# Attention, mixture of experts and MLP in one kernel: laying out keys and queries once per pair of heads

## The chip, the cores and the metric

The kernel runs as one program on one core of a Trainium2 chip. The metric is the device time of one execution in microseconds. The profile is of one execution, and its times are counted from the first instruction of the program (the span).

## What is computed

Three layers follow one another. The first is what the change is about: attention over 4 batches of 8 heads with 1152 keys and half as many queries, since neighbouring queries are averaged first.

```
q, k, v: (4, 8, 1152, 64) float32
q_pool = q.reshape(B, H, S // 2, 2, D).mean(axis=3)
scores = matmul(q_pool, k.T) / sqrt(D)
attn   = exp(scores - max(scores)); attn /= sum(attn) + 1e-9
out    = matmul(attn, v)
```

Its output, heads side by side, is x (4, 576, 512). Then x goes through four attention experts of 64 columns each (causal, with weights wq, wk, wv, wo and a gate that picks two of the four), and at last through a mixing step with U and V and an MLP of 512 to 2048 to 512 with residual.

## The kernel before

**Pairs.** Two heads are handled together, their 2 x 64 columns side by side on the 128 partitions: 16 pairs in all. For a pair, `prep` (L499) makes what its scores need. `load_q`, `load_k`, `load_v` (L477 to L497) fetch raw rows into `qr`, `kr`, `vr`. `pool_q` adds neighbouring queries on VectorE (DVE). `tr_q` turns the queries on TensorE (PE) in two pieces (4 and 2 transposes), `tr_k` the keys in three pieces of three transposes. Each turned piece is split into a high part (`qh`, `kn`, by ScalarE, ACT) and a remainder (`ql`, `klo`, by DVE). `evac_q_all` (L383) and `evac_k` (L354) then copy the parts by DMA, piece by piece, into the operands of the score matmuls: keys into `s1a, s1b, s2a, s2b`, queries into `q1a, q1b, q2a, q2b`, and the queries also into `bd`, a block-diagonal form. A class `Pair` holds the eight score operands; there are two Pairs, for even and odd pairs of heads, and two each of `bd` and `kn`. A row maximum is needed before the scores: `mxs` (L527) multiplies `bd` by `kn` on PE (27 matmuls per pair) and reduces each on DVE into `mp`; `fin` (L540) turns the maxima and puts them by small DMAs (`nm`, L423) into a row of `q2a` and `q2b`, once for queries 0 to 319 and once for the rest.

**Steps.** `attend` (L53) writes the order by hand for PE, DVE and ACT. A pair has 18 units (2 halves of the queries x 9 key tiles), a unit two steps: 36 steps per pair. A step issues two score matmuls (L566, L567) and the exponential on ACT (L568, `pt`). Every third unit the value matmuls (L586) of earlier units follow. GpSimd (POOL) sums the `pt` tiles (L578). Into these steps, by the numbers of the tables at L20 to L27, the preparation of the next pair is placed: number 0 is the first step of the pair that runs just before, number 36 the first of the pair itself. What a step returns as a function is run one step later.

**Queues.** All DMAs are issued by one engine, SP, one after another. Their order is not written by hand: a scheduler sets it, from the order of the code and its own estimate of when their inputs are ready. If an instruction at SP's head waits, all that stand behind it wait.

**Weights.** `expert_weights` (L256) loads the experts' weights into halves of one staging tile `stg` (L278 to L321) and cuts them into high and low parts (`cut`, L226: ACT, then DVE). The six loads are spread over the odd pairs 1, 3, 5, 7, 9, 11: the load at step 7 of the pair (`WL_AT`), the cuts at steps 17 and 29 and, where there are more than two, again in the next pair (`WC_AT`).

**First and last pair.** Before the loop, all of pair 0's preparation is run by `run_all` (L611), in the order of its numbers; pair 1's is placed into the first steps of pair 0 (L626). During the last pair the first expert's preparation takes the free places (L893 to L895): the pool of the attention's right side is closed, four cuts of x (`xh`, `xl`, L227 and L228) and 15 steps of projections (L669) and maxima are spread evenly from step 12 on.

After the attention come the experts (same structure, 8 pairs of batch and expert pair) and the MLP (L922 to L1052), neither of which the change edits beyond renaming an argument.

Of the kernel before, what the change touches and what calls it, by code (L numbers as in the profile page):

```python
# [18 lines left out]

GROUP = 3  # L20
POOL_AT, LQ_AT, LK_AT, V_AT = -13, -48, -24, 6
Q_AT = [-1, 5]
K_AT = [-1, 5, 11]
M_AT = [1, 2, 3, 6, 7, 8, 9, 12, 13, 14, 15, 16, 18, 19, 20, 21, 22, 24, 25, 26, 27, 30, 31, 32, 33, 36, 37]
F_AT = [23, 41]

WL_AT, WC_AT = 7, [17, 29]  # L27


CUT_AT = [0, 0, 0, 0]  # L30
# [98 lines left out]
def kernel(  # L129
# [45 lines left out]
    def f(ap):  # L175
        return ap.bitcast(F32)
# [177 lines left out]
    def evac_k(klo, ps, kn, pr, sl):  # L354


        nc.scalar.activation(kn[:, sl], ps, AF.Copy)

        def rest():
            nc.vector.tensor_sub(klo, ps, f(kn[:, sl]))  # L360
            for a in range(2):
                for h in range(2):
                    nc.sync.dma_start(f(pr.S1[a][HALF[h], sl]), f(kn[HALF[a], sl]))
                nc.sync.dma_start(f(pr.S2[a][HALF[a], sl]), f(klo[HALF[a]]))

        return rest

    def evac_q(ps, bd, pr, sl, done):
        t0, nt = sl.start // 64, (sl.stop - sl.start) // 64
        for a in range(2):  # L370
            nc.scalar.activation(pr.Q1[a][HALF[a], sl], ps[HALF[a]], AF.Copy)

        def rest():
            for a in range(2):
                nc.vector.tensor_sub(pr.Q1[a][HALF[1 - a], sl], ps[HALF[a]], f(pr.Q1[a][HALF[a], sl]))
                nc.sync.dma_start(f(pr.Q2[a][HALF[a], sl]), f(pr.Q1[a][HALF[a], sl]))
                nc.scalar.activation(bd[HALF[a], t0:t0 + nt, HALF[1 - a]],
                                     ps[HALF[a]].rearrange("p (t j) -> p t j", j=64), AF.Copy)
            done()

        return rest

    def evac_q_all(qh, ql, ps, bd, pr, sl, done):  # L383


        t0, nt = sl.start // 64, (sl.stop - sl.start) // 64
        nc.scalar.activation(qh, ps, AF.Copy)

        def rest():
            nc.vector.tensor_sub(ql, ps, f(qh))  # L390
            for a in range(2):
                r = HALF[a]
                nc.sync.dma_start(f(bd[r, t0:t0 + nt, r]), f(qh[r]).rearrange("p (t j) -> p t j", j=64))
            for a in range(2):
                r = HALF[a]
                nc.sync.dma_start(f(pr.Q1[a][r, sl]), f(qh[r]))
                nc.sync.dma_start(f(pr.Q1[a][HALF[1 - a], sl]), f(ql[r]))
                nc.sync.dma_start(f(pr.Q2[a][r, sl]), f(qh[r]))
# [100 lines left out]
    def prep(i):  # L499
# [9 lines left out]
        def tr_k(c):  # L509
            kr = kraw[i]  # L510
            ps = pst.tile([P, 512], F32, name="st") if i == 0 else pms.tile([P, 512], F32, name="ms")
            for j in range(3):
                nc.tensor.transpose(ps[:, j * P:(j + 1) * P], kr[:, 3 * c + j, :, :], ident)
            sl = slice(c * 384, c * 384 + 384)
            own["k", c, i % 2] = i
            return evac_k(per_r.tile([P, 384], F32R, name="klo", bufs=2), ps[:, :384], KN[i % 2], pr, sl)

        def tr_q(j0, j1):
            ps = pms.tile([P, 512], F32, name="ms")
            n = (j1 - j0) * 96  # L520
            for j in range(j0, j1):
                nc.tensor.transpose(ps[:, (j - j0) * 96:(j - j0 + 1) * 96], st["qp"][:, j, :, :],
                                    ident[:96, :96])
            qh, ql = (per_r.tile([P, 384], F32R, name=nm) for nm in ("qh", "ql"))
            return evac_q_all(qh[:, :n], ql[:, :n], ps[:, :n], BD[i % 2], pr, slice(j0 * 96, j1 * 96), lambda: own.update({(t, i % 2): i for t in range(j0 * 96 // 64, j1 * 96 // 64)}))

        def mxs(t, c):  # L527
            assert own[t, i % 2] == i and own["k", c, i % 2] == i
# [24 lines left out]
    def unit(i, u):  # L553
# [51 lines left out]

        return score, pv, (post_a, post_r, post_b) if kt == NKT - 1 else None

    load_q(0)
    load_k(0)
    load_v(0)  # L610
    run_all(sorted(prep(0), key=lambda x: x[0]))  # L611
    n = 4 * NKT
    for x, (load, steps) in enumerate(expert_weights()):
        place(side, [(WL_AT, load)], n * (1 + 2 * x))
        at = [y + n * w for w in range(2) for y in WC_AT]
        place(side, list(zip(at, steps)), n * (1 + 2 * x))
        assert len(steps) <= len(at)
    for i in range(NP):
        units += [unit(i, u) for u in range(2 * NKT)]
    for i in range(1, NP):  # L620
        n0 = (i - 1) * n
        for at, g in ((LQ_AT, load_q), (LK_AT, load_k), (V_AT, load_v)):
            side.setdefault(max(3 * i - 3, n0 + at), []).append(lambda g=g, i=i: g(i))
        for at, g in prep(i):
            if i == 1:
                at = max(at, 2 if at == POOL_AT else 5 if at in Q_AT + K_AT else 6)  # L626
            side.setdefault(n0 + at, []).append(g)
# [83 lines left out]
    def prep_b(j, what):  # L711
# [372 lines left out]
```

## Time and profile before

| | |
|---|---|
| median of 3 runs | 1261.41 us (1260.43 to 1265.64) |
| the profiled execution | 1257.52 us, span 1255.7 us |
| before the first exponential | 36.1 us |
| attention, first full score to the last pair's end | about 35.5 to 594.6 us |
| PE busy | 1141.4 us, 91% of the span |
| DVE, ACT, POOL busy | 61%, 37%, 39% |
| DMA | 120.06 MB, mean 96 GB/s |

A pair's start is read in the timeline as its first score matmul (L566; 36 of them make a pair); from pair to pair that gives the stretches used below. A busy PE is not PE at its peak, since matmuls overlap, so the idle time of PE in a stretch says more than its busy share. The column PEclk is the mean granted clock of TensorE in the stretch, 1.00 being 2.4 GHz.

### The profile page before, as it was taken

The numbers are of one execution on the slowest core, as the hardware profiler recorded it, in microseconds if no ns is written. First come the engines' busy times: TensorE is split into PE (matmuls) and PEld (weight loads), VectorE is DVE, ScalarE is ACT, GpSimd is POOL, SyncE is SP. The second block draws the span as 40 slices with busy tenths as digits, with TensorE's granted clock in tenths as the row PEclk, the third lists the DMA queues.
The fourth block names the chain that finished last, engine by engine and source line by source line (L and its number), as shares of the span: only waits on it lengthen the run. The fifth ranks groups of instructions, "written<-read, shape, count | busy, mean of one in ns | idle before, by whom it ended". The sixth has DMA issues, their size and how long they took to land.

```text
span 1255.7 us, 19444 instructions
## 1 busy us (share of the span) xinstructions
PE 1141.4 (91%) x6748; PEld 909.8 (72%) x6748; DVE 766.8 (61%) x1661; ACT 468.0 (37%) x1184; POOL 488.1 (39%) x382
## 2 busy tenths in 40 slices
PE   4696999798989788998999999999999999999998
PEld 3474676566767566766877777578897898998987
DVE  5264676477778568665675858998849228222222
ACT  1253455355545445554445454542221112111110
POOL 4274777477767657784222212421112003000000
PEclk9997999899999989998999999999999999999999
DMA  7556666647575656521120404435303002000111
GB/s 172 123 122 141 156 147 148 145 115 182 128 177 138 157 116 149 137 65 39 39 65 13 110 5 114 135 122 206 101 18 110 8 1 68 1 1 1 51 51 50
DMA packets 140000, 120.06 MB, mean 96 GB/s; under 512 B 76288, under 2 KB 123392, under 8 KB 139904
## 3 DMA queue, kind: packets, MB, share of 16 engines
q1 hardware_dynamic: 139904, 118.84, 37.5%
q8 instruction: 53, 0.87, 0.3%
q14 instruction: 43, 0.35, 0.1%
HBM read 52.65 MB, written 9.44 MB: 49 GB/s over the span
## 4 chain that ended last, share of the span: by engine, by line
PE 56%; DVE 19%; issue 11%; DMA 6%; ACT 3%; SPq 3%; POOL 1%; ACTq 0%; DVEq 0%; POOLq 0%
PE ms L990 9%; PE pv L586 9%; PE o L1001 8%; PE ms L669 6%; PE st L566 5%; PE ms L533 5%; PE st L567 4%; DVE mp L535 3%; DMA bd<-qh 2%; PE pv L817 2%; DVE dca L238 1%; DVE dcb L246 1%; ACT pt L568 1%; DVE dca L241 1%; PE st L792 1%
## 5 line engine op out<-in xcount | busy, mean ns | idle before, releaser
L578 POOL TENSOR_TENSOR acc<-acc,pt 128x576 f32<-128x576 f32 x224 | 326.7, 1459 | 102.2 <-ACT pt L568 75.4
L568 ACT ACTIVATE pt<-st 128x288 f32<-128x288 f32 x576 | 218.0, 409 | 213.2 <-PE st L567 197.0
L535 DVE TENSOR_REDUCE mp<-ms 128x1 f32<-128x384 f32 x432 | 213.9, 547 | 69.0 <-PE ms L533 68.8
L990 PE MATMUL ms<-uh,w 128*128 128x384 f32 x768 | 214.4, 340 | 0.8 <-DVE hl L994 0.8
L533 PE MATMUL ms<-kn,bd 128*128 128x384 f32 x432 | 156.9, 374 | 45.8 <-DVE mp L535 18.0
L1001 PE MATMUL o<-w,hh 128*128 128x512 f32 x576 | 182.1, 396 | 2.1 <-ACT hh L993 2.1
L994 DVE SCALAR_TENSOR_TENSOR hl<-ms,hh 128x384 fp32r<-128x384 f32 x96 | 53.4, 556 | 199.2 <-ACT hh L993 198.8
L586 PE MATMUL pv<-pt,vr 128*64 128x288 f32 x1152 | 165.9, 425 | 0.0
L990 PEld LDWEIGHTS ms<-uh,w 128*128 128x128 f32 x768 | 140.9, 188 | 6.0 <-DVE hl L994 1.0
L993 ACT ACTIVATE hh<-ms 128x384 fp32r<-128x384 f32 x96 | 46.8, 489 | 262.7 <-PE ms L990 262.7
L990 PE MATMUL ms<-ul,w 128*128 128x384 f32 x384 | 129.7, 338 | 2.2 <-DVE ul L228 2.2
L533 PEld LDWEIGHTS ms<-kn,bd 128*128 128x128 f32 x432 | 85.7, 199 | 59.6 <-DVE mp L535 29.0
L228 POOL TENSOR_TENSOR w<-dcb,w 128x512 fp32r<-128x512 f32 x32 | 43.7, 1369 | 214.8 <-ACT w L227 206.5
L586 PEld LDWEIGHTS pv<-pt,vr 128*64 128x64 f32 x1152 | 79.3, 141 | 59.0 <-issue 16.1
L1001 PEld LDWEIGHTS o<-w,hh 128*128 128x128 f32 x576 | 106.8, 188 | 21.0 <-ACT hh L993 3.4
L1001 PE MATMUL o<-w,hl 128*128 128x512 f32 x288 | 114.2, 396 | 1.7 <-DVE hl L994 1.7
L566 PE MATMUL st<-q1b,s1b 128*128 128x288 f32 x288 | 88.1, 306 | 18.3 <-ACT pt L568 18.2
L566 PE MATMUL st<-q1a,s1a 128*128 128x288 f32 x288 | 98.6, 342 | 0.7 <-ACT pt L568 0.7
L566 PEld LDWEIGHTS st<-q1a,s1a 128*128 128x128 f32 x288 | 55.6, 193 | 46.0 <-issue 42.2
L567 PE MATMUL st<-q2a,s2a 128*128 128x288 f32 x288 | 86.7, 301 | 1.8 <-issue 1.8
L567 PE MATMUL st<-q2b,s2b 128*128 128x288 f32 x288 | 86.9, 302 | 0.0
L809 POOL TENSOR_TENSOR acc<-acc,pt 128x576 f32<-128x576 f32 (+4 forms) x48 | 44.2, 920 | 108.8 <-ACT pt L800 104.7
(169 smaller groups left out, 1890.9 us busy)
## 6 DMA issues: line engine op xcount, KB each, us to landing
raw<-in_moe_w_ch_dram SPq DMA_DIRECT2D x32, 512.0 KB
qr<-in_q_dram SPq DMA_DIRECT2D x16, 576.0 KB
vr<-in_v_dram SPq DMA_DIRECT2D x16, 576.0 KB
s1a<-kn SPq DMA_DIRECT2D x96, 96.0 KB
s1b<-kn SPq DMA_DIRECT2D x96, 96.0 KB
kr<-in_k_dram SPq DMA_DIRECT2D x30, 288.0 KB
s2a<-klo SPq DMA_DIRECT2D x48, 96.0 KB
s2b<-klo SPq DMA_DIRECT2D x48, 96.0 KB
```

The lines of the kernel that those rows point to most:

```text
L533: nc.tensor.matmul(ps[:, :384], BD[i % 2][:, t, :], KN[i % 2][:, c * 384:c * 384 + 384], start=True, stop=True)
L535: nc.vector.tensor_reduce(st["mp"][:, t, c:c + 1], ps[:, :384], axis=X, op=ALU.max)
L566: nc.tensor.matmul(ps[:, :HT], pr.S1[a][:, ks], pr.Q1[a][:, qs], start=True, stop=False)
L567: nc.tensor.matmul(ps[:, :HT], pr.S2[a][:, ks], pr.Q2[a][:, qs], start=False, stop=True)
L568: nc.scalar.activation(c["pt"][:, a, :], ps[:, :HT], AF.Exp, scale=0.0625)
L578: nc.gpsimd.tensor_add(acc[i, h], acc[i, h], c["pt"])
L586: nc.tensor.matmul(o[64 * a:64 * a + 64, :HT], vr[:, a, kt, :], c["pt"][:, a, :], start=(kt == 0), stop=(kt == NKT - 1))
L669: nc.tensor.matmul(ps, stat[x][s], mov[x][m], start=(x == 0 and y == 0), stop=(x == n - 1 and y == 2))
L990: nc.tensor.matmul(ps[:, :TB], W[fi][:, 0, a, cs], m[:, c, :], start=(c == 0 and y == 0), stop=(c == NC - 1 and y == 2))
L993: nc.scalar.activation(h, ps[:, :TB], AF.Relu)
L994: nc.vector.scalar_tensor_tensor(l, ps[:, :TB], 0.0, f(h), op0=ALU.max, op1=ALU.subtract)
L1001: nc.tensor.matmul(o[s_], hl[m][:, r], W[fi][:, 1, a, :], start=(fi % FG == 0 and y == 0), stop=(fi % FG == FG - 1 and y == 2))
```

## The change

Four things are edited.

1. **Layout once per pair.** `evac_q_all` is gone. `qh`, `ql` and `klo` become tiles of a whole pair (576, 576 and 1152 columns, one buffer each) in place of pieces of 384. A turned piece now only goes to its staging tile and, for the queries, to `bd`. A new step `lay` at number 13 copies the whole tiles into the eight score operands: 12 DMAs of 64 rows where there were 30. Per pair SP issues 24 DMAs instead of 42: 4 to `bd`, 12 of layout, 4 `nm`, 4 loads (before: 4, 30, 4, 4). The bytes are the same.
2. **Queries turned earlier.** `Q_AT` goes from -1 and 5 to -7 and -1. The first maxima (`M_AT`) start at number 3 instead of 1.
3. **Weight loads.** A load is placed at step 31 of the even pair before, 12 steps earlier than at step 7 of the odd one. The cuts stay where they were.
4. **First and last pair.** Before the loop all turns of pair 0 come first, then the loads of pair 1's keys and queries, then the layout and maxima, then pair 1's own steps with negative numbers. Pair 1's other steps stand at their normal numbers. In the last pair the projections stand at written numbers (`XP_AT`, from 18 on) instead of evenly spread (from 16 on).

```diff
-Q_AT = [-1, 5]
+Q_AT = [-7, -1]
 K_AT = [-1, 5, 11]
-M_AT = [1, 2, 3, 6, 7, 8, 9, 12, 13, 14, 15, 16, 18, 19, 20, 21, 22, 24, 25, 26, 27, 30, 31, 32, 33, 36, 37]
+LAY_AT = 13
+M_AT = [3, 4, 6, 7, 8, 9, 10, 12, 13, 14, 15, 16, 18, 19, 20, 21, 22, 24, 25, 26, 27, 30, 31, 32, 33, 36, 37]
-WL_AT, WC_AT = 7, [17, 29]
+WL_AT, WC_AT = 31, [17, 29]
+XC_AT = [12, 13, 14, 15]
+XP_AT = [18, 19, 21, 22, 25, 26, 27, 28, 29, 30, 31, 32, 33, 34, 35]
...
         def rest():
-            nc.vector.tensor_sub(klo, ps, f(kn[:, sl]))
-            for a in range(2):
-                for h in range(2):
-                    nc.sync.dma_start(f(pr.S1[a][HALF[h], sl]), f(kn[HALF[a], sl]))
-                nc.sync.dma_start(f(pr.S2[a][HALF[a], sl]), f(klo[HALF[a]]))
+            nc.vector.tensor_sub(klo[:, sl], ps, f(kn[:, sl]))
+            if pr:
+                lay_k(klo, kn, pr, sl)
...
+    def lay_k(klo, kn, pr, sl):
+        for a in range(2):
+            for h in range(2):
+                nc.sync.dma_start(f(pr.S1[a][HALF[h], sl]), f(kn[HALF[a], sl]))
+            nc.sync.dma_start(f(pr.S2[a][HALF[a], sl]), f(klo[HALF[a], sl]))
...
-            return evac_k(per_r.tile([P, 384], F32R, name="klo", bufs=2), ps[:, :384], KN[i % 2], pr, sl)
+            return evac_k(klo, ps[:, :384], KN[i % 2], None, sl)
...
-            qh, ql = (per_r.tile([P, 384], F32R, name=nm) for nm in ("qh", "ql"))
-            return evac_q_all(qh[:, :n], ql[:, :n], ps[:, :n], BD[i % 2], pr, slice(j0 * 96, j1 * 96), lambda: own.update({(t, i % 2): i for t in range(j0 * 96 // 64, j1 * 96 // 64)}))
+            if j0 == 0:
+                st["q"] = [per_r.tile([P, T], F32R, name=nm) for nm in ("qh", "ql")]
+            qh, ql = st["q"]
+            sl = slice(j0 * 96, j1 * 96)
+            nc.scalar.activation(qh[:, sl], ps[:, :n], AF.Copy)
+
+            def rest():
+                nc.vector.tensor_sub(ql[:, sl], ps[:, :n], f(qh[:, sl]))
+                for a in range(2):
+                    nc.sync.dma_start(f(BD[i % 2][HALF[a], sl.start // 64:sl.stop // 64, HALF[a]]),
+                                      f(qh[HALF[a], sl]).rearrange("p (t j) -> p t j", j=64))
...
+        def lay():
+
+            qh, ql = st["q"]
+            for a in range(2):
+                nc.sync.dma_start(f(pr.Q1[a][HALF[a]]), f(qh[HALF[a]]))
+                nc.sync.dma_start(f(pr.Q1[a][HALF[1 - a]]), f(ql[HALF[a]]))
+                nc.sync.dma_start(f(pr.Q2[a][HALF[a]]), f(qh[HALF[a]]))
+            lay_k(klo, KN[i % 2], pr, slice(0, S))
...
+    P0, P1 = (sorted(prep(x), key=lambda y: y[0]) for x in range(2))
+    turns = Q_AT + K_AT + [POOL_AT]
     load_q(0)
     load_k(0)
+    run_all([x for x in P0 if x[0] in turns])
+    load_k(1)
+    load_q(1)
     load_v(0)
-    run_all(sorted(prep(0), key=lambda x: x[0]))
+    run_all([x for x in P0 if x[0] not in turns and x[0] < F_AT[1]])
+    run_all([x for x in P1 if x[0] < 0])
+    run_all([x for x in P0 if x[0] == F_AT[1]])
     for x, (load, steps) in enumerate(expert_weights()):
-        place(side, [(WL_AT, load)], n * (1 + 2 * x))
-        at = [y + n * w for w in range(2) for y in WC_AT]
-        place(side, list(zip(at, steps)), n * (1 + 2 * x))
+        place(side, [(WL_AT, load)], n * 2 * x)
+        at = [y + n * w for w in range(1, 3) for y in WC_AT]
+        place(side, list(zip(at, steps)), n * 2 * x)
...
-    steps = sum(prep_b(0, "s"), [])
-    place(side, [(12 + x * (n - 13) / len(steps), g) for x, g in enumerate(steps)], n * (NP - 1))
+    for at, steps in zip((XC_AT, [], XP_AT), prep_b(0, "s")):
+        place(side, list(zip(at, steps)), n * (NP - 1))
```

Where the instructions stand, at the three places that matter. First SP's queue in pair 1, up to the load of the first weights `wq` (four DMAs) into `stg`. Before, from the end of pair 0:

```order
L480 DMA qr<-in_q_dram 96x2x768
L278 DMA stg<-in_moe_wq_dram 128x4x64
L393 DMA bd_135<-qh 64x6x64 x2
...
L363 DMA s1b_142<-kn_139 64x384 x2
L364 DMA s2b_144<-klo 64x384
L496 DMA vr<-in_v_dram 128x2x576
L278 DMA stg<-in_moe_wq_dram 128x4x64 x3
L363 DMA s1a_141<-kn_139 64x384 x2
L364 DMA s2a_143<-klo 64x384
```

With the change:

```order
L469 DMA qr<-in_q_dram 96x2x768
L522 DMA bd_135<-qh 64x6x64 x2
L282 DMA stg<-in_moe_wq_dram 128x4x64 x4
L522 DMA bd_135<-qh 64x3x64 x2
L532 DMA q1a_145<-qh 64x576
L533 DMA q1a_145<-ql 64x576
L411 DMA q2a_161<-nm 1x4x64
```

Before, 31 DMAs of the next pair's `bd` and layout, of `nm` and of `vr` stand between the first and the second DMA of the weights; now all four stand together, ahead of the layout of the pair after.

Second, SP's queue in the same pair from the values' load on, with the change (before, the layout there came in pieces of 64x384 and 64x192, as above):

```order
L485 DMA vr<-in_v_dram 128x2x576
L534 DMA q2a_147<-qh 64x576
L478 DMA kr<-in_k_dram 128x9x64 x2
L532 DMA q1b_146<-qh 64x576
L533 DMA q1b_146<-ql 64x576
L534 DMA q2b_148<-qh 64x576
L373 DMA s1a_141<-kn_139 64x1152 x2
L374 DMA s2a_143<-klo 64x1152
L373 DMA s1b_142<-kn_139 64x1152 x2
L374 DMA s2b_144<-klo 64x1152
L411 DMA q2a_147<-nm 1x5x64
```

The next keys' load `kr` now stands ahead of the keys' layout, where before it stood behind the last piece of it; the maxima `nm` stand behind the whole layout in both.

Third, PE's queue before the loop, up to pair 0's first scores. Before:

```order
L533 MATMUL ms<-kn_139,bd_135 128x384 x10
L418 MATMUL ms<-ident,mx 4x128
L567 MATMUL st<-q2a_147,s2a_143 128x288
...
L522 MATMUL ms<-ident,qp 128x96 x6
L513 MATMUL ms<-ident,kr 128x128 x6
L586 MATMUL pv<-pt,vr 64x288 x2
```

With the change:

```order
L543 MATMUL ms<-kn_139,bd_135 128x384 x10
L576 MATMUL st<-q1a_145,s1a_141 128x288
L511 MATMUL ms<-ident,qp 128x96 x6
L502 MATMUL ms<-ident,kr 128x128 x3
L406 MATMUL ms<-ident,mx 4x128
L577 MATMUL st<-q2a_147,s2a_143 128x288
```

Pair 1's six query transposes and its first three key transposes, which stood behind the first scores of pair 0, now stand ahead of them.

## Rows read from the trace of the kernel before

**Rows 1.** The page: busy time of each engine, share of the span, instructions.

```profile
PE 1141.4 (91%) x6748; PEld 909.8 (72%) x6748; DVE 766.8 (61%) x1661; ACT 468.0 (37%) x1184; POOL 488.1 (39%) x382
```

**Rows 2.** Windows: stretch, length, engines' busy time (instructions), PEclk, DMA share, GB/s.

```profile
0.00:17.00 17.00, 2.79 (x13) 2.42 (x13) 4.92 (x15) 3.24 (x5) 14.18 (x25) 1.00 0.95 209
35.50:550.20 514.70, 445.92 (x2924) 330.01 (x2924) 343.64 (x690) 249.83 (x684) 346.33 (x239) 0.96 0.61 142
35.50:79.90 44.40, 34.71 (x188) 26.26 (x188) 19.64 (x39) 17.17 (x45) 21.73 (x15) 0.96 0.56 124
79.90:123.50 43.60, 31.66 (x199) 22.81 (x197) 22.84 (x47) 17.23 (x47) 23.19 (x16) 0.84 0.59 133
156.60:186.40 29.80, 29.05 (x198) 21.65 (x196) 23.39 (x47) 17.41 (x47) 22.50 (x15) 0.99 0.62 148
218.90:260.10 41.20, 31.46 (x198) 22.80 (x196) 22.95 (x47) 17.12 (x47) 21.79 (x15) 0.88 0.61 142
354.90:384.70 29.80, 28.67 (x199) 21.47 (x197) 24.89 (x50) 16.17 (x45) 21.25 (x15) 1.00 0.67 155
416.10:458.50 42.40, 30.89 (x199) 22.48 (x197) 24.71 (x49) 16.27 (x45) 23.07 (x16) 0.88 0.55 126
522.50:550.20 27.70, 27.56 (x191) 20.64 (x189) 19.11 (x42) 15.57 (x43) 20.58 (x15) 1.00 0.48 119
```

**Rows 3.** Waits, whole span: engine line waited for, us in total, times, longest.

```profile
PE ms L513 <- DMA kr<-in_k_dram: 13.0, 6, 3.0
PE ms L533 <- DMA bd<-qh: 12.8, 6, 7.5
ACT qh L387 <- DMA q2b<-qh: 12.2, 4, 8.7
ACT wqk L227 <- DMA stg<-in_moe_wq_dram: 12.2, 1, 12.2
DVE stg L237 <- DMA stg<-in_moe_V_dram: 10.4, 1, 10.4
ACT wvg L227 <- DMA stg<-in_moe_w_gate_dram: 9.5, 1, 9.5
```

**Rows 4.** Timeline of SP, 36 to 130 us: start, length, what, [idle before].

```profile
71.70 0.43 SPq L278 DMA_DIRECT2D stg<-in_moe_wq_dram  x1
78.64 1.38 SPq L393 DMA_DIRECT2D bd<-qh  x2
...
97.66 1.24 SPq L363 DMA_DIRECT2D s1b<-kn  x2
98.95 0.60 SPq L364 DMA_DIRECT2D s2b<-klo  x1
99.64 0.53 SPq L496 DMA_DIRECT2D vr<-in_v_dram  x1
100.22 1.59 SPq L278 DMA_DIRECT2D stg<-in_moe_wq_dram  x3
```

**Rows 5.** Timeline of ACT in pair 1, the cut of wq.

```profile
106.20 0.63 ACT L227 ACTIVATE wqk<-stg 128x512 fp32r<-128x512 f32 x1 [12.16 <-DMA stg<-in_moe_wq_dram]
```

**Rows 6.** The page's DMA queue: packets, MB, share of 16 engines' span.

```profile
q1 hardware_dynamic: 139904, 118.84, 37.5%
```

**Rows 7.** The keys' tile: weight loads of its transposes, ns min/median/max.

```profile
L513 PEld LDWEIGHTS ms<-ident,kr x135: 137/140/230, 41.8 to 530.5; 128*128 128x128 f32 x135
```

**Rows 8.** The chain that ended last, first 50 us: start, length, what.

```profile
9.12 7.94 DMA bd<-qh
...
28.81 4.29 DVE mp L535 x9
...
33.71 1.79 issue
35.50 0.58 PE st L567
...
38.11 8.23 DMA qr<-in_q_dram
46.37 2.11 DMA q2b<-qh
```

**Rows 9.** Timeline of DVE in the last pair: the cuts of x.

```profile
561.01 5.10 DVE L228 TENSOR_TENSOR xl<-xt,xh 128x576 fp32r<-128x576 f32 x3 [2.00 <-ACT pt L568]
```

**Rows 10.** The page's costliest groups: busy, mean ns | idle before, releaser.

```profile
L578 POOL TENSOR_TENSOR acc<-acc,pt 128x576 f32<-128x576 f32 x224 | 326.7, 1459 | 102.2 <-ACT pt L568 75.4
L568 ACT ACTIVATE pt<-st 128x288 f32<-128x288 f32 x576 | 218.0, 409 | 213.2 <-PE st L567 197.0
```

More of the change, by code (lines that the diff above doesn't have):

```diff
@@ L378, in rest @@
                                      ps[HALF[a]].rearrange("p (t j) -> p t j", j=64), AF.Copy)
[L379 to L398, printed above, removed]
             done()
@@ L473 @@
     prs = [Pair(per_r, 0, S, T, True), Pair(per, 1, S, T, True)]
+    klo = per_r.tile([P, S], F32R, name="klo")
     NP = B * H // 2
@@ L523, in tr_q @@
                                     ident[:96, :96])
-            qh, ql = (per_r.tile([P, 384], F32R, name=nm) for nm in ("qh", "ql"))
-            return evac_q_all(qh[:, :n], ql[:, :n], ps[:, :n], BD[i % 2], pr, slice(j0 * 96, j1 * 96), lambda: own.update({(t, i % 2): i for t in range(j0 * 96 // 64, j1 * 96 // 64)}))
+            if j0 == 0:
[8 more added lines that the diff above has]
+                                      f(qh[HALF[a], sl]).rearrange("p (t j) -> p t j", j=64))
+                own.update({(t, i % 2): i for t in range(sl.start // 64, sl.stop // 64)})
+            return rest
+        def lay():
[5 more added lines that the diff above has]
+            lay_k(klo, KN[i % 2], pr, slice(0, S))
         def mxs(t, c):
@@ L547, in prep @@
         steps += [(at, lambda c=c: tr_k(c)) for c, at in enumerate(K_AT)]
-        steps += [(at, lambda x=x: mxs(*x)) for at, x in zip(M_AT, order)]
+        steps += [(LAY_AT, lay)] + [(at, lambda x=x: mxs(*x)) for at, x in zip(M_AT, order)]
         return steps + [(at, lambda x=x: fin(*x)) for at, x in zip(F_AT, BLOCKS)]
@@ L606, in unit @@
         return score, pv, (post_a, post_r, post_b) if kt == NKT - 1 else None
+    n = 4 * NKT
+    P0, P1 = (sorted(prep(x), key=lambda y: y[0]) for x in range(2))
+    turns = Q_AT + K_AT + [POOL_AT]
     load_q(0)
     load_k(0)
+    run_all([x for x in P0 if x[0] in turns])
+    load_k(1)
+    load_q(1)
     load_v(0)
-    run_all(sorted(prep(0), key=lambda x: x[0]))
-    n = 4 * NKT
+    run_all([x for x in P0 if x[0] not in turns and x[0] < F_AT[1]])
+    run_all([x for x in P1 if x[0] < 0])
+    run_all([x for x in P0 if x[0] == F_AT[1]])
     for x, (load, steps) in enumerate(expert_weights()):
-        place(side, [(WL_AT, load)], n * (1 + 2 * x))
-        at = [y + n * w for w in range(2) for y in WC_AT]
-        place(side, list(zip(at, steps)), n * (1 + 2 * x))
+        place(side, [(WL_AT, load)], n * 2 * x)
+        at = [y + n * w for w in range(1, 3) for y in WC_AT]
+        place(side, list(zip(at, steps)), n * 2 * x)
         assert len(steps) <= len(at)
@@ L622 @@
         for at, g in ((LQ_AT, load_q), (LK_AT, load_k), (V_AT, load_v)):
[L623 to L627, printed above, removed]
+            if i > 1 or g is load_v:
+                side.setdefault(max(0, n0 + at), []).append(lambda g=g, i=i: g(i))
+        place(side, [x for x in (P1 if i == 1 else prep(i)) if n0 + x[0] >= 0], n0)
     bes = xes.enter_context(ExitStack())
@@ L654, in open_left @@
         bt["wk"] = pool(bes, "bwk", 1)
-    GT, own = {}, {}
+    GT = {}
     def rows(t):
@@ L725, in project @@
             own["k", c0 > 0] = j
-            return evac_k(bt["klo"][:, sl], ps[:, :c1 - c0], bt["kn"], pr, sl)
+            return evac_k(bt["klo"], ps[:, :c1 - c0], bt["kn"], pr, sl)
         def mxs(t):
```

## The prediction
> **What bounds the kernel now.** I read the page first. PE is busy for 91% of the span, far ahead of every other engine [rows 1], so the question is where PE still waits, stage by stage. The windows show it for the attention [rows 2]: pairs 0 to 14 take 514.7 us, an average of 34.3, with a granted clock of 0.96. The reader should compare the rows of single pairs. Pair 14 takes 27.7 us and PE idles in it for 0.1. Pairs 3 and 9 take 29.8, with 0.8 and 1.1 idle. Pairs 1, 5 and 11 take 43.6, 41.2 and 42.4 with the same instructions (198 or 199 on PE), 10 to 12 of it idle, and their clock is 0.84 to 0.88 where the calm pairs have 0.99 to 1.00. The work of a pair is thus some 28.5 us of PE, and what lies above is waiting.
>
> The waits say for what [rows 3]. The three long ones are cuts of expert weights: ACT 12.2 us for wq, ACT 9.5 for the gate that is loaded after wv, DVE 10.4 for V; they fall in pairs 1, 5 and 11. Next to them stand PE waits for `kr` (13.0 in 6 cases) and `bd` (12.8 in 6), and ACT waits for `q2b<-qh` (12.2 in 4), that is, for the single `qh` piece that the layout DMAs are still reading.
>
> SP's timeline tells why these DMAs are late [rows 4]. The first DMA of wq was issued at 71.7 us; then, from 78.6 on, come 31 layout and other DMAs, about 0.6 us each with hardly a pause, and the remaining three of wq go out at 100.2. The cut starts at 106.2, after 12.16 us of idle ACT [rows 5]. Nothing was slow but the queue. A layout DMA of 96 KB (98.3 kB) is issued in 0.59 to 0.62 us [rows 4]. The page gives 118.84 MB in 37.5% of the span on all 16 engines [rows 6], which is 252 GB/s while they work, or 0.39 us for those 98.3 kB. So while layouts are issued SP is the bound, not the wires. A pair has 42 DMAs: 42 x 0.6 = 25 us of SP in a pair of 30.
>
> **The change part by part.** *Layout once per pair.* Removed are 30 layout DMAs, added 12: SP needs 24 x 0.6 = 14 us per pair. The bytes stay: 6 x 288 KB of keys, 6 x 144 of queries, 288 to `bd`, 3 x 576 of loads, together 4608 KB or 4.72 MB, at 252 GB/s 18.7 us of a 29 us pair, so the wires don't become the bound. `kr` is now queued ahead of the key layout, and its reader comes 23 steps after its issue step; I take its wait as gone. The query turns move from steps -1 and 5 to -7 and -1: 6 steps, some 5 us, more between `bd`'s DMA and its first matmul (which itself moves two steps back), against the 2.11 us from issue to landing of a layout DMA with a free way [rows 8]; I take this wait as gone too. The whole `qh` has no reader left when the next pair writes it, 16 steps after `lay`. On PE, ACT and DVE the edit moves instructions and adds none, so there it costs nothing unless their new place delays a score.
>
> What remains per pair is PE's own work: pair 14's 27.7, which has no turns of a later pair at its end. These are seven transposes at 0.14 us [rows 7], 1.0 us, and I leave 0.3 for the last waits on DVE. That is **29.0 us**, and pairs 3 and 9, with 28.7 and 29.05 busy, say the same. Ten pairs (2 to 4, 6 to 10, 12, 13) take 514.7 - 44.4 - 127.2 - 27.7 = 315.4 now and 290.0 then: **-25.4**. Bounds: 28.2 each (-8 more), or 29.8, the calm pairs of today (+8).
>
> Here the Trainium skill speaks against the edit. Its page "DMA: Bandwidth & Descriptors", section "Issuing engines are not separate DMA queues", calls the time on the sequencer to start a DMA usually small beside the DMA itself; by that, 18 issues fewer per pair would buy nothing, the 25.4 us would be zero and the sum below 1202; the first rival is this case. The trace disagrees for this size: 0.6 us of issue against 0.39 of transfer.
>
> *Weight loads.* A load now stands 12 steps (10 us) earlier and, by SP's order, in one piece ahead of the layout. It has 22 steps, about 18 us, until its cut; 512 KB take 2.1 us at 252 GB/s. The three waits go, and with them the slower clock after them: pairs 1, 5 and 11 go from 127.2 to 3 x 29.0 = 87.0, **-40.2**. Of pair 1's excess a part is the late start of its own steps, which the last edit removes. The other side: the load now stands between the two `bd` pieces, 4 issues or 2.4 us of SP; the second piece is wanted 22 steps later, which hides it. Bounds: each of the three could keep 2 us (+6).
>
> *First pair.* Before the first score stand `bd`'s landing (7.94 us after issue, behind 1.7 MB of loads, at 209 GB/s in that stretch) and the 27 maxima on DVE, nine of which took 4.29 us, 0.48 each [rows 2, 8]. The loads ahead of `bd` stay in the order, so the maxima still begin near 17.9. Between them stand 1.9 us less of other DVE work (the second `qp`, `ql`, `klo` go ahead of them), so they end near 31.4 instead of 33.3. Then came 1.79 us of waiting for `nm`, which stood behind 30 layout DMAs [rows 8]; now the first `nm` stands behind 12. In its place PE makes pair 1's turns, under DVE's last maxima. Layout and pair 1's keys, 3.3 MB, need 13 us at 252 GB/s after 17, so they land near 32. First scores at 32.7 instead of 35.5: **-2.8**. Bounds: -4, or +5 if the wires run at only the 160 GB/s at which SP feeds layouts today (98.3 kB in 0.61 us).
>
> Pair 0 takes 44.4, of which PE idles about 10: a load (8.23) and then `q2b` (2.11) hold ACT's single `qh` [rows 8]. Pair 1's queries are then already turned and `qh` is whole. I take 29.0 plus 1.5 for `bd` landing just in time and a cold clock: 30.5, **-13.9**. Bounds: 29 to 35.
>
> *Last pair.* PE waits for three `xl` of 1.7 us each, slowed by POOL beside them [rows 9]; two more steps of scores now stand before the first projection. I take **-2.0**, bounds 0 to -4.
>
> **Sum:** -25.4 - 40.2 - 2.8 - 13.9 - 2.0 = -84.3 against the profiled execution's 1257.5: 1173.2. That execution is 3.9 us under the median of 1261.4, so I add 3.9: **1177 us**.
>
> **The rivals.** *The calm pairs stay as they are.* If their waits have another cause than SP's issues, only the known stalls go, and the stalled pairs come down to the others' 31.5: 1261.4 - 2.8 - 13.9 - 2.0 - (127.2 - 3 x 31.5 = 32.7) gives 1210. For it: DVE is busy 23 to 25 us in calm pairs, the next to fill up, and ACT also waits for PE. Against it: pair 14, and that 13.0 + 12.8 + 12.2 us of waits are for DMAs [rows 3]. Neither POOL (16 sums of 1.46 us, 23.3) nor ACT (36 x 0.41, 14.7 plus turns) reaches 29 [rows 10]. 8%.
>
> *The weight waits return.* If the loads, though earlier, are not landed 22 steps later, 32 us come back: 1209. Against it stands SP's order. 4%.
>
> *Slower: the layout burst is late in every pair.* The layout can't be complete until the last key piece is turned, step 12, and the scores want all of it at step 36: 24 steps of 0.8 us, 19.3 us. Behind step 12 the queue holds 2592 KB of layout, 1152 KB of `kr` and `vr`, in three pairs the weights' 512 KB: up to 4.35 MB, 17.3 us at 252 GB/s and 2.1 to land. That is exactly the slack. Below 252 GB/s every pair starts late: at 209, 3.5 us times 14 pairs, which leaves 1226; at 160 GB/s 9.9 us each, or 1316. It is slower than before below about 187 GB/s, where 6 us a pair eat the 84. Against it: most query layouts can start near step 0, `vr` is issued near step 6, so the full 4.35 MB stand together in few pairs, and long rows should not move slower than short ones. The Trainium skill, same page, section "Queues, rings and completion order", has each DMA engine take its descriptors in ring order, so the small `nm` and `bd` wait behind a burst; the trace agrees (7.94 us for `bd` behind loads). 4%.
>
> **How the numbers follow.** A measurement of this kernel can tell about 0.5%, 6.3 us, from no change. The forecast has 82%, the three rivals 8, 4 and 4, and 2 are left to mixed cases near no change. Its own bounds: pairs at 28.2 (-10), the first pair and start at their best (-3), the last -2 give 1162; pairs at 29.8 (+10) with the start +5, pair 0 +4, and half of the rest give 1202. Both ends are kept; they leave out the two rivals at 1210 and the slower one. Faster by over 0.5%: 93%, within 3%, slower 4%.
>
> **What would show it.** Right: pairs of 28 to 30 us all through, no window of 40; no wait of ACT or DVE for `stg`; waits for `kr` and `bd` under 3 us in total; first full score near 33; DMA share in the attention near 0.65 with fewer packets. Wrong: PE waiting at a pair's first scores for `s2` or `q2` (the burst), or PE waiting for DVE's `mp` for over 2 us a pair (the first rival).

## The result, and the profile after

The changed kernel takes 1169.45 us (median of 4 runs, 1167.22 to 1174.48) against 1261.82 in the runs beside it: a ratio of 0.927 with a 95% interval of 0.923 to 0.931, 7.3% less. The forecast was 1177, with 1162 to 1202 as its range. The profiled execution took 1167.44 us, 90.1 less than the one of before. Stretch by stretch, profile against profile, in us:

| stretch | before | after | difference | forecast |
|---|---|---|---|---|
| up to the first full score | 35.5 | 32.4 | -3.1 | -2.8 |
| pair 0 | 44.4 | 28.0 | -16.4 | -13.9 |
| pairs 1, 5, 11 | 127.2 | 88.2 | -39.0 | -40.2 |
| the ten other pairs (2 to 13) | 315.4 | 288.3 | -27.1 | -25.4 |
| pair 14 | 27.7 | 27.2 | -0.5 | 0 |
| last pair | 44.4 | 38.9 | -5.5 | -2.0 |
| experts and MLP | 661.1 | 662.7 | +1.6 | 0 |
| sum | | | -90.0 | -84.3 |

The windows of the changed kernel show it (columns as in [rows 2]): pairs 0, 1 and 5, the two longest (11, 12) and the last pair.

```profile
32.40:60.40 28.00, 27.14 (x182) 20.73 (x181) 19.21 (x38) 16.75 (x44) 21.75 (x15) 0.97 0.87 192
60.40:89.40 29.00, 28.73 (x199) 21.52 (x197) 23.85 (x47) 17.51 (x47) 23.95 (x17) 1.00 0.74 169
174.40:203.40 29.00, 28.72 (x198) 21.49 (x196) 23.84 (x47) 17.54 (x47) 23.96 (x17) 1.00 0.71 164
347.60:377.80 30.20, 29.01 (x199) 21.55 (x197) 26.66 (x49) 16.61 (x45) 22.93 (x17) 1.00 0.70 158
377.80:408.70 30.90, 28.98 (x198) 21.46 (x196) 26.61 (x48) 17.02 (x46) 23.84 (x17) 1.00 0.65 153
464.10:503.00 38.90, 34.09 (x228) 24.36 (x226) 22.93 (x46) 19.86 (x53) 28.67 (x23) 1.00 0.13 31
```

Not all of the difference is waiting. The attention as a whole, from the first full score to the end of the last pair, before and after:

```profile
35.50:594.60 559.10, 483.54 (x3150) 356.39 (x3150) 367.60 (x738) 269.91 (x737) 374.82 (x261) 0.95 0.57 133
32.40:503.00 470.60, 459.12 (x3142) 344.19 (x3141) 370.04 (x734) 270.81 (x735) 376.76 (x261) 1.00 0.69 157
```

Of the 88 us between the two, PE's idle time gives 64 (75.6 against 11.5), and 24 are busy time of the same matmuls. The mean granted clock went from 0.95 to 1.00; the lower clock of before stands in the pairs with a long stall (0.84 and 0.88 in [rows 2]).

Pair 1, which took 43.6 with 12 of it idle and a granted clock of 0.84, is now one of 29.0 with 0.3 idle at 1.00. Its SP queue explains it. The timeline of SP in pair 1 (start, length, what):

```profile
60.62 0.55 SPq L532 DMA_DIRECT2D q1a<-qh  x1
...
72.09 1.50 SPq L373 DMA_DIRECT2D s1a<-kn  x2
73.69 1.19 SPq L374 DMA_DIRECT2D s2a<-klo  x1
74.91 2.74 SPq L373 DMA_DIRECT2D s1b<-kn  x2
77.70 0.83 SPq L374 DMA_DIRECT2D s2b<-klo  x1
```

The whole layout of pair 2 is issued between 60.6 and 78.5, and its first scores stand at 89.4, 11 us after the last issue. By the trace's DMA records its last row of 4608 bytes has moved at 83.1, so some 6 us are to spare; over the pairs 1 to 15 it is 4.8 to 12.5. Where [rows 4] showed hardly a pause, SP now has free stretches. The cut of wq, which began at 106.20 after 12.16 us of waiting [rows 5], has no wait at all and stands 13 us after its pair's start instead of 26. From the timeline of ACT:

```profile
73.37 0.62 ACT L231 ACTIVATE wqk<-stg 128x512 fp32r<-128x512 f32 x1
```

Of the waits of [rows 3], those for `kr`, `q2b<-qh` and the three for `stg` are not in the list any more. What is left for DMAs near there, and one wait that is new in its size (engine line waited for, us in total, times, longest):

```profile
ACT pt L578 <- POOL acc L588: 24.4, 15, 1.6
...
DVE qp L495 <- DMA qr<-in_q_dram: 7.8, 2, 4.4
...
PE ms L543 <- DMA bd<-qh: 7.3, 2, 6.5
...
ACT qh L517 <- DMA q2a<-nm: 5.3, 1, 5.3
```

Of `bd`'s 7.3, the 6.5 end at 16.5 us, before any score; in the pairs 0.85 is left, once. ACT's 5.3 for `qh` stand once too, before the first full score, where pair 1's queries are turned. The page's engine line and DMA queue:

```profile
PE 1119.7 (96%) x6748; PEld 900.2 (77%) x6748; DVE 771.3 (66%) x1661; ACT 469.7 (40%) x1184; POOL 490.0 (42%) x382
...
q1 hardware_dynamic: 116864, 118.82, 41.3%
```

The bytes are those of [rows 6], the packets fewer by a sixth. 41.3% of 1165.7 us is 481 us of all engines, 37.5% of 1255.7 was 471: the wires did not get faster. What went is time in which they had nothing to do. Two windows of 10 us in which SP issues with hardly a pause show it, before (15 issues, see [rows 4]) and after (9 issues, the end of the layout above):

```profile
84.00:94.00 10.00, 10.00 (x71) 7.50 (x73) 6.46 (x15) 6.20 (x18) 7.91 (x6) 1.00 0.44 103
72.00:82.00 10.00, 10.00 (x70) 7.71 (x71) 9.05 (x18) 6.55 (x18) 9.37 (x6) 1.00 1.02 222
```

Before, the DMA engines were busy for 0.44 of that time (103 GB/s) while SP had no time left; now they are full (1.02, since a transfer counts in the window where it starts).

### The profile page after: what moved, and what is told of

Same layout as the page of the kernel before. It is cut to its first block, busy times and chain, and to the rows that moved or that the text cites. A ratio compares the mean times of both kernels' runs of the same rounds, so it can differ in the third digit from the quotient of the medians.

```text
span 1165.7 us, 18965 instructions
## 1 busy us (share of the span) xinstructions
PE 1119.7 (96%) x6748; PEld 900.2 (77%) x6748; DVE 771.3 (66%) x1661; ACT 469.7 (40%) x1184; POOL 490.0 (42%) x382
## 3 DMA queue, kind: packets, MB, share of 16 engines
q1 hardware_dynamic: 116864, 118.82, 41.3%
## 4 chain that ended last, share of the span: by engine, by line
PE 65%; DVE 17%; issue 11%; DMA 3%; ACT 2%; POOL 1%; SPq 1%; ACTq 0%; DVEq 0%; POOLq 0%
PE pv L596 10%; PE ms L1005 10%; PE o L1016 9%; PE ms L684 7%; PE st L576 7%; PE ms L543 5%; PE st L577 5%; PE pv L832 2%; DVE mp L545 2%; DVE dcb L250 1%; DVE dca L242 1%; PE ms L502 1%; DVE dca L245 1%; PE ms L603 1%; PE st L807 1%
## 5 line engine op out<-in xcount | busy, mean ns | idle before, releaser
L543 PE MATMUL ms<-kn,bd 128*128 128x384 f32 x432 | 151.7, 361 | 13.2 <-DMA bd<-qh 7.3
L596 PE MATMUL pv<-pt,vr 128*64 128x288 f32 x1152 | 159.3, 412 | 0.0
L596 PEld LDWEIGHTS pv<-pt,vr 128*64 128x64 f32 x1152 | 76.9, 136 | 54.9 <-issue 9.8
L543 PEld LDWEIGHTS ms<-kn,bd 128*128 128x128 f32 x432 | 83.7, 194 | 21.4 <-DVE mp L545 12.0
```

The costliest lines, as they stand in the source:

```text
L543: nc.tensor.matmul(ps[:, :384], BD[i % 2][:, t, :], KN[i % 2][:, c * 384:c * 384 + 384], start=True, stop=True)
L596: nc.tensor.matmul(o[64 * a:64 * a + 64, :HT], vr[:, a, kt, :], c["pt"][:, a, :], start=(kt == 0), stop=(kt == NKT - 1))
```

## The experiments

Eleven edited kernels and the changed one once more, in four groups; each group shares its runs of the kernel before, whose medians lay between 1259.5 and 1265.6. The theory of the forecast: SP's issues are the bound, and their number is cut. Its rivals: the weight loads' place alone does it, the early turns alone do it, or the wires are the bound and long rows made them faster. The early turns alone in the kernel before were not run; what they are worth is read from taking them out and from adding them to the layout.

**Loads moved, nothing else** (in the kernel before).

```diff
-WL_AT, WC_AT = 7, [17, 29]
+WL_AT, WC_AT = 31, [17, 29]
...
-        place(side, [(WL_AT, load)], n * (1 + 2 * x))
+        place(side, [(WL_AT, load)], n * 2 * x)
...
```

> The kernel before, with only the weight loads placed 12 steps earlier (SP still issues 42 DMAs a pair). If the three long waits were a matter of the loads' place in SP's queue, they go and the stalled pairs 1, 5 and 11 come down from 42 to the other pairs' 31.5 us: 1262 - 33 = 1229 us, with pair 1 perhaps keeping some because its own steps start late. If an overfull queue is the cause, the load only pushes the other DMAs back and the waits turn up at bd, kr or the layout: 1245 us or more.

Measured: 1238.15 us, ratio 0.983 (0.979 to 0.987), between the two figures. Pairs 1, 5 and 11 came down to 31.5, 33.3 and 34.5, 28 us less in sum, but other waits grew. The waits of this run:

```profile
PE ms L533 <- DMA bd<-qh: 21.4, 9, 8.0
...
PE ms L513 <- DMA kr<-in_k_dram: 13.8, 6, 3.1
...
ACT qh L387 <- DMA stg<-in_moe_wq_dram: 7.7, 1, 7.7
```

`bd` went from 12.8 to 21.4. The queue is as long as it was, and what is moved up in it pushes back something else.

**Loads put back** (in the changed kernel, as in all that follow unless said otherwise).

```diff
-WL_AT, WC_AT = 31, [17, 29]
+WL_AT, WC_AT = 7, [17, 29]
...
-        place(side, [(WL_AT, load)], n * 2 * x)
+        place(side, [(WL_AT, load)], n * (1 + 2 * x))
...
```

> The changed kernel, with the weight loads back at step 7 of the odd pair, 10 steps ahead of their cut. If the queue's length was the cause, a load now has at most a few DMAs ahead of it, lands within the 8 us, and the time stays within 5 us of 1169. If it is the 12 steps that matter, the waits of ACT and DVE for the staging tile return, about 10 us in each of pairs 1, 5 and 11: near 1200 us.

Measured: 1173.09 us, 0.931 (0.928 to 0.934), with no wait for `stg`; pairs 1 to 14 agree with those of the changed kernel within 0.4 us each. With a short queue the place of the loads is worth at most the 3 to 4 us between the medians (the changed kernel, run again below, takes 1170.2), which the pairs don't show.

**Layout in pieces again**, with the whole staging tiles, the early turns and everything else kept: 42 issues per pair.

```diff
-LAY_AT = 13
+LAY_AT = 2
...
-            return evac_k(klo, ps[:, :384], KN[i % 2], None, sl)
+            return evac_k(klo, ps[:, :384], KN[i % 2], pr, sl)
...
+            for c in (slice(0, 384), slice(384, T)):
...
```

The keys' pieces are laid out at their turn, the queries' two pieces in a loop over `c` at step 2.

> The changed kernel, with the layout again in 30 pieces issued as the pieces are turned (keys) or from step 2 on (queries): 42 DMAs a pair, same bytes, whole staging tiles and early query turns kept. If SP's issue time was the bound, a pair needs 25 us of SP and the calm pairs go back from 28.5 towards 31 us, with waits for bd, kr or nm: 1169 + 14 x 2 to 2.5 = 1195 to 1205 us. If the places of the steps and the whole staging tiles made the gain, the count does nothing: 1169 to 1175 us.

Measured: 1202.71 us, 0.955 (0.951 to 0.959): 33 us lost with the same bytes and the same computation. Its waits:

```profile
PE ms L543 <- DMA bd<-qh: 12.4, 9, 6.8
...
PE ms L502 <- DMA kr<-in_k_dram: 8.1, 7, 2.5
...
PE st L577 <- DMA q2a<-nm: 7.5, 4, 3.9
```

and its SP in pair 2, one after another with hardly a pause:

```profile
111.52 0.59 SPq L533 DMA_DIRECT2D q1b<-qh  x1
112.16 0.59 SPq L534 DMA_DIRECT2D q1b<-ql  x1
112.80 0.60 SPq L535 DMA_DIRECT2D q2b<-qh  x1
```

with the DMA engines less than half busy in that stretch:

```profile
105.00:115.00 10.00, 10.00 (x72) 7.44 (x69) 8.22 (x16) 5.32 (x15) 6.97 (x6) 1.00 0.41 96
```

The waits for `bd`, `kr` and `nm` are back with the number of issues; those for `stg` are not. The pieces also go out at other steps than the whole layout did, but an SP that issues with hardly a pause to DMA engines that are 0.41 busy is short of issue time and not of wires. That part of the theory is shown.

**Queries turned late again.**

```diff
-Q_AT = [-7, -1]
+Q_AT = [-1, 5]
-M_AT = [3, 4, 6, 7, 8, 9, 10, 12, 13, ...]
+M_AT = [1, 2, 3, 6, 7, 8, 9, 12, 13, ...]
```

> The changed kernel, with the query turns back at steps -1 and 5 and the maxima back at step 1 (12 layout DMAs kept). If the early turns are needed beside the short queue, PE waits at step 1 of every pair for bd, which needs at least 1.3 us of issue and 2.1 us to land after step 0: 1 to 2 us a pair, 1185 to 1200 us. If the short queue alone does it, bd lands in time and the time stays within 6 us of 1169.

Measured: 1194.36 us, 0.948 (0.944 to 0.952), 25 us lost. Pairs of 28 and 29 become 29 to 34, and PE waits again:

```profile
PE ms L543 <- DMA bd<-qh: 19.0, 9, 5.9
...
PEld ms L543 <- DVE mx L548: 14.8, 11, 1.9
...
PE ms L543 <- DVE mx L548: 6.2, 7, 0.9
```

5.9 of `bd`'s 19.0 are the start; the other eight waits, 13.1 us, are in the pairs. In the pairs that don't wait for `bd` there, PE's maxima wait some 0.9 us for DVE (`mx`, where the row maxima of the preparation before are put together), a wait that the changed kernel doesn't have at that line. So the two tables together were a cost of their own; how much of it is the late turns and how much the early maxima, this run doesn't tell apart.

**The layout alone** (in the kernel before: only whole staging tiles and 12 layout DMAs at step 13).

```diff
-Q_AT = [-7, -1]
+Q_AT = [-1, 5]
-WL_AT, WC_AT = 31, [17, 29]
+WL_AT, WC_AT = 7, [17, 29]
...
-    run_all([x for x in P0 if x[0] in turns])
...
+    run_all(sorted(prep(0), key=lambda x: x[0]))
```

(Against the changed kernel; the old `M_AT` and the old spread in the last pair too.)

> The kernel before with the layout part alone: whole staging tiles and 12 layout DMAs at step 13; turns, maxima, weight loads, first and last pair as before. If the shorter queue is the main cause, this alone takes the weight waits away and most of the gain is here: undoing the rest cost 25 (turns), 3 (loads), 6 (last pair) and perhaps 5 to 15 us (first pair), so 1205 to 1220. If the parts need each other, the waits for the staging tile or bd remain and it stays above 1230.

Measured: 1201.42 us, 0.952 (0.949 to 0.954): 59 of the 91 us, more than expected. Pairs 1, 5 and 11 take 30.5, 30.2 and 31.4 with the weight loads at their old place, and nothing waits for `stg`.

```profile
PEld ms L543 <- DVE mx L548: 17.6, 14, 1.7
...
PE ms L543 <- DMA bd<-qh: 11.5, 6, 5.3
...
PE ms L502 <- DMA kr<-in_k_dram: 3.5, 1, 3.5
```

What is left in the pairs are short waits for `bd` and for DVE's maxima, as in the run before.

**The layout and the early turns** (the run above with two tables of the change).

```diff
-Q_AT = [-1, 5]
+Q_AT = [-7, -1]
-M_AT = [1, 2, 3, 6, 7, 8, 9, 12, 13, ...]
+M_AT = [3, 4, 6, 7, 8, 9, 10, 12, 13, ...]
```

> The layout from whole staging tiles together with the early turns of the queries (Q_AT -7 and -1, maxima from step 3), with the loads, the first pair and the last pair as in the kernel before. If the layout and the turns are the two causes and the other three edits have the small prices that taking them out showed (loads 3 or less, first pair 6 to 7, last pair 6), this run takes 1183 to 1188 us, about 14 above the changed kernel, with pairs 2 to 14 at 28 to 31 us and no wait for stg. If the edits depend on one another further (the loads or the first pair being needed for the turns' gain), it stays at 1192 or above, nearer to the layout alone at 1201.

Measured: 1182.08 us, 0.938 (0.935 to 0.940), 19 us below the layout alone. Pairs 1 to 14 agree with the changed kernel's within 0.4 us each. What remains to the changed kernel is 12.6 us by the medians; in the profiles 8.0 lie in the first pair (pair 1 starts at 68.4 instead of 60.4) and 4.3 in the last (43.2 instead of 38.9).

**The old order of the first pair.**

```diff
-    run_all([x for x in P0 if x[0] in turns])
-    load_k(1)
-    load_q(1)
     load_v(0)
+    run_all(sorted(prep(0), key=lambda x: x[0]))
...
+            if i == 1:
+                at = max(at, 2 if at == POOL_AT else 5 if at in Q_AT + K_AT else 6)
```

> The changed kernel with the order before the loop and in pair 0 as it was. The forecast gave the start 2.8 and pair 0 13.9 us; measured were 3.1 and 16.4. If the new order made them, the time is 1169 + 17 to 20 = 1186 to 1189; if most came from the whole query tile and the short queue, which stay, PE in pair 0 no longer waits for the q2b copy and the time is 1172 to 1178.

Measured: 1176.72 us, 0.934 (0.932 to 0.936). The first full score stands even earlier, at 29.9 us, but pair 1 starts at 65.6, after a wait of 4.2 us for its keys; in two profiles of the changed kernel it starts at 60.4 and 61.9. The new order is worth 4 to 5 us there and 6 to 7 by the medians, not the 16.7 that the forecast put under the first pair.

**The last pair spread evenly again.**

```diff
-    for at, steps in zip((XC_AT, [], XP_AT), prep_b(0, "s")):
-        place(side, list(zip(at, steps)), n * (NP - 1))
+    steps = sum(prep_b(0, "s"), [])
+    place(side, [(12 + x * (n - 13) / len(steps), g) for x, g in enumerate(steps)], n * (NP - 1))
```

> The changed kernel with the last pair's projections spread evenly again from step 16 on. The last pair came down from 44.4 to 38.9 us, 5.5 where 2.0 were forecast. If the new numbers made all of that, it is back at 44 and the time at 1175; if the numbers made only the 2 us and the rest came with PE's clock and the calmer pair before, the time is 1171.

Measured: 1176.03 us, 0.930 (0.928 to 0.932). Beside it the changed kernel was run again, with no edit:

> The changed kernel once more, beside the next three on one chip: 1169 us, within 4.

Measured: 1170.21 us (1166.87 to 1173.87), 0.925 (0.923 to 0.928). So the written numbers are worth some 6 us by the medians; in the profiles the last pair goes from 43.1 to 38.9.

**The layout 18 steps later**, to see the burst that the third rival feared.

```diff
-LAY_AT = 13
+LAY_AT = 31
```

> The changed kernel with the layout step at 31 instead of 13, so that the last key copies go out some five steps before the scores that read them. In the changed kernel a pair's layout was issued in 15 us and done some 10 us before its scores. If that slack is real, 18 steps (14 us) later makes the copies 3 to 4 us late in every pair, with PE waiting for s1b, s2b or nm at a pair's first scores: 1169 + 14 x 2 to 4 = 1197 to 1225. If the scheduler sends them as early as before, or if the wires are much faster than 252 GB/s, the time stays within 10 us of 1169.

Measured: 1221.9 us, 0.968 (0.965 to 0.970). Waits for the layout itself appear:

```profile
DVE klo L364 <- DMA s2b<-klo: 41.3, 13, 5.7
...
PE st L576 <- DMA s1b<-kn: 10.8, 6, 2.3
...
PE st L577 <- DMA s2b<-klo: 4.9, 6, 1.6
```

PE's first scores of a pair wait for `s1b` and `s2b`, and DVE for the single `klo` that the layout is still reading. By the DMA records the last layout row now moves 0.5 to 4.3 us after the first score of the pairs 1 to 11. The burst is real; at step 13 it has the room it needs. The longest of these waits is DVE's, so the 52 us lost are those of a late layout and of the single `klo` together, not of the burst alone.

**Cuts of the weights at step 5**, for what the pairs 9 to 12 still lose.

```diff
-WL_AT, WC_AT = 31, [17, 29]
+WL_AT, WC_AT = 31, [5, 29]
```

The reason was read in the changed kernel's timelines in pair 9: on DVE the decoding of weights (L241, L242) stands between the maxima,

```profile
301.71 1.00 DVE L545 TENSOR_REDUCE mp<-ms 128x1 f32<-128x384 f32 x2
302.63 0.72 DVE L241 TENSOR_SCALAR stg<-stg 128x160 int32<-128x160 int32 x1
303.38 1.47 DVE L242 TENSOR_SCALAR stg<-stg 128x160 f32<-128x160 f32 x1
304.77 1.47 DVE L545 TENSOR_REDUCE mp<-ms 128x1 f32<-128x384 f32 x3
```

and PE waits for them:

```profile
305.37 0.44 PE L543 MATMUL ms<-kn,bd 128*128 128x384 f32 x1 [0.75 <-DVE mp L545]
```

> The changed kernel with the weight cuts of step 17 moved to step 5, where DVE is idle for 1.1 us. Pairs 9 to 12 take 29.3, 29.7, 30.2 and 31.0 us where their neighbours take 28.0 to 29.0; if DVE's cuts between the maxima make the difference, they come to 28.0 to 29.2 and the time falls by 4 to 6 us to 1164. If the cause is the next pair's other work, nothing changes. The other side: 10 steps may be too short for the load, and ACT waits for the staging tile, +5 to +10.

Measured: 1164.9 us (1163.55 to 1165.88), 0.921 (0.919 to 0.923), the fastest of all. Pairs 9 to 12 take 28.1, 28.5, 29.0 and 29.8 instead of 29.3, 29.7, 30.2 and 31.0. Its window of pair 12, the longest left:

```profile
375.10:404.90 29.80, 28.81 (x199) 21.68 (x197) 25.64 (x48) 16.99 (x46) 24.07 (x17) 1.00 0.68 160
```

**The cuts of x earlier as well** (on top of the last one).

```diff
-XC_AT = [12, 13, 14, 15]
+XC_AT = [7, 8, 9, 10]
...
-    place(side, [(11, open_right)], n * (NP - 1))
+    place(side, [(6, open_right)], n * (NP - 1))
```

> The one before, and in the last pair the right side's pool closed at step 6 instead of 11 and the four cuts of x from step 7 instead of 12, so that they are done when the first projection comes at step 18. If PE's wait there (1.9 us for xl) and ACT's delay were the cuts', another 2 to 3 us fall: 1161. If closing the pool earlier only waits for the pair's last maxima, no change.

Measured: 1167.24 us, 0.924 (0.921 to 0.925): a miss. PE's wait for `xl` is gone, but the last pair takes 41.7 instead of 38.9, with 6.2 us of it idle on PE where the run before had 3.5. ACT's timeline there:

```profile
472.18 0.44 ACT L435 ACTIVATE d<-d 128x288 f32<-128x288 f32 x1 [3.78 <-DVE d L431]
472.53 0.99 ACT L578 ACTIVATE pt<-st 128x288 f32<-128x288 f32 x3
```

and DVE's, ahead of the step that ACT waits for:

```profile
464.55 6.75 DVE L232 TENSOR_TENSOR xl<-xt,xh 128x576 fp32r<-128x576 f32 x4 [4.19 <-ACT xh L231]
...
471.93 0.22 DVE L431 RECIPROCAL d<-d 128x9 f32<-128x9 f32 x1
```

The four cuts of x hold DVE for 6.75 us; the row sums (`d`) stand behind them, ACT waits 3.78 us for `d`, the exponentials (`pt`) stand behind that instruction on ACT, and PE waits for them.

## Why the prediction was right

**The bound** was read rightly. The forecast put 0.6 us of SP on each DMA and 42 of them against a pair of 30 us. With 24 the waits for `kr`, `q2b`, `stg` and, but for the start, `bd` are gone; with 42 and all else kept those for `kr` and `bd` return, waits for `nm` come beside them, and 33 us are lost. One size was off: the 24 issues of pair 1 take 18.7 us together, 0.78 each, not 24 x 0.6 = 14, since in the burst an issue takes up to 2.1 us while the DMA engines are full. The Trainium skill, "DMA: Bandwidth & Descriptors", section "Issuing engines are not separate DMA queues", which calls the time to start a DMA usually small beside the DMA, does not hold for this size: the traces have 0.59 us of issue for 98.3 kB, which at the 231 GB/s worked out below take an estimated 0.43, and the DMA engines are only 0.41 to 0.44 busy in the two windows above in which SP issues such DMAs.

**Ten calm pairs**: 29.0 was forecast, the mean is 28.8. The floor read from pair 14 was right, though the pairs do not all lie within the 28 to 30 us that were to show it: 11 and 12 take 30.2 and 31.0, and the run with the cuts at step 5 takes 1.2 off each. The first rival (pairs stay at 31.5, 1210 us) is refuted by the windows.

**Weight loads**: the number was right (-40.2 against -39.0), the cause was booked too narrowly. The step of the forecast that failed is the one that put this whole sum under "A load now stands 12 steps (10 us) earlier". The load's move alone took 28 us out of these pairs and 22 out of the kernel, since other waits grew; the layout alone, with the loads at their old place, brought the three pairs to 92.1, 35 less. Either edit removes the three waits of the cuts; beside the short queue the move adds nothing that the pairs show. The second rival (the weight waits return) did not come about.

**First pair**: -16.7 was forecast, for the new order and the whole `qh` in one sum; -19.5 came, but taking the order back costs only 4 to 7. The rest doesn't need the order: by the layout and the early turns alone pair 1 starts at 68.4 where it started at 79.9.

**Last pair**: the mechanism was right, its price was luck in part, and a term was left out. -2.0 was forecast for the wait for `xl`, 5.5 measured. The windows of the last pair before, and of the run with the even spread:

```profile
550.20:594.60 44.40, 37.62 (x228) 26.38 (x226) 23.95 (x48) 20.08 (x53) 28.48 (x23) 0.88 0.11 27
465.40:508.50 43.10, 36.36 (x227) 25.69 (x225) 24.22 (x47) 20.09 (x53) 28.44 (x22) 0.92 0.12 28
```

PE idles 6.8 us in the first, 6.7 in the second (3.2 for `xl`, 1.4 for `acc`, 1.1 for `bdb`, the rest in smaller waits) and 4.8 in the changed kernel (1.9 for `xl`, 2.1 for `pt`): the changed kernel has 2 us less of idle time, the size that was forecast. Of the wait that the forecast named, `xl`, 1.3 went; that the others make it 2.0 is luck. The other 3.5 us are PE's busy time, 37.6, 36.4 and 34.1, with a granted clock of 0.88, 0.92 and 1.00. The forecast counted the slower clock in the pairs 1, 5 and 11 and not in this one.

**The slower rival** had a real mechanism, but in every pair from pair 1 on at least 4.8 us of slack stood against it. It shows with the layout at step 31, where it and the wait for `klo` cost 52 us together, still not enough to be slower than before.

**Smaller things.** Of the signs that were named, waits for `bd` under 3 us did not come: they are 7.3, of which 6.5 stand before the first score, where the edit leaves the loads ahead of `bd`. The upper end of the range, 1202, adds up to 1200 by the terms given for it (10, 5, 4 and half of 6 + 2). And the DMA share was forecast near 0.65 at 252 GB/s; pair 5 has 0.71. Its 164 GB/s / 0.71 are 231 GB/s while the engines work. The attention's row in [rows 2] had 142 / 0.61 = 233 to read; the page's 252 is a mean over the span, with the experts and the MLP in it.

So the sum came out right while two of its terms stood, in whole or in part, under the wrong edits, because the edits overlap. Built up from the kernel before, the layout gives 59 us, the early turns (with the later maxima) 19 more, the other three edits together 13 more. Taken out of the changed kernel one at a time, they cost 33 (layout in pieces), 25 (turns), at most 3 to 4 (loads), 6 to 7 (first pair, by the medians) and 6 (last pair). The layout alone gives 59, all the rest without it 57 (1202.71 against 1260.04), both together 91: some 25 us are there for either, and the weight waits, worth 22 by the loads' move alone, are the likely bulk of it. That last point is worked out, not tried by itself.

## What to carry to other kernels

Count, for each period of the loop, the issues on the queue that issues DMAs and multiply by the issue time in its timeline; if that nears the period, waits show up at several unrelated tiles, and shortening the queue removes them together, while moving one entry forward pushes back another. Before you book a wait to the edit that touches it, ask whether an earlier edit removes it already: two kernels, one with each edit alone, tell that. Count the clock with a stall of PE: 24 of the 88 us here were busy time. When a step is moved earlier on one in-order engine, look at what then stands behind it on that engine, and at the engines that wait for that.

## What was not expected of the hardware

**Issue time did not grow with size.** On a free stretch the key layout of 64 x 1152 (288 KB) was issued as fast as the one of 64 x 384 (96 KB) in [rows 4], 1.24 us for two. SP before pair 0's scores, changed kernel:

```profile
19.13 0.59 SPq L534 DMA_DIRECT2D q2b<-qh  x1
19.83 1.18 SPq L373 DMA_DIRECT2D s1a<-kn  x2
21.10 0.77 SPq L374 DMA_DIRECT2D s2a<-klo  x1
21.91 3.02 SPq L373 DMA_DIRECT2D s1b<-kn  x2
```

The last two took 1.5 us each, so a large burst is not issued at that speed to its end. From 19 to 25 us the DMA engines are full (share 1.03, 246 GB/s), which may be what holds SP there; it was not tried.

**The start depends on when TensorE's clock rises, which differs between executions of one kernel.** In the profiled execution above PE's score matmuls of 288 columns follow one another every 0.24 us up to 34 us and every 0.13 from 35.5 on; in the second profile of the same kernel they stand 0.24 apart until 38.9, and pair 0 ends 1.5 us later (61.9 against 60.4). That is 1.5 of the 4.4 us between the spans of these two profiles; the other 2.9 lie behind the attention. The clock column shows the lower level in the first profile only, 0.50 (1.2 GHz):

```profile
17.00:32.40 15.40, 14.66 (x39) 9.06 (x38) 13.85 (x32) 1.47 (x4) 0.00 (x0) 0.50 0.86 188
```

In the second it reads 1.00 for the same stretch, with the same wide spacing:

```profile
17.00:32.00 15.00, 14.26 (x38) 8.81 (x37) 13.72 (x31) 1.37 (x4) 0.00 (x0) 1.00 0.90 192
```

The Trainium skill, page "TensorE: Matmul & The Clock Gate", section "Wait — 56ns, not 53.3ns?", has matmuls start at the lower level one after another at their columns divided by 1.2 GHz; for 288 columns that is 0.24 us, as both traces show. So ahead of the first change of clock in a trace, the spacing of equal matmuls is the surer sign.

**POOL is near.** It is busy for 22 to 24 us of a pair of 28 to 29, and ACT now waits for its sums about once a pair (24.4 us in 15 cases; before, for one of 2.0 us). ACT's idle time covers it for now.
